# q in longer runs and another token order from batch 3 on, with an order of blocks 2 to 8 written out by hand: linear attention followed by a PReLU feed-forward layer

## The chip, the cores and the metric

The kernel runs on one core of a Trainium2 chip. The metric is the device time of one execution in microseconds (us); given are the median and the extremes of several runs. Five engines work side by side: TensorE (PE, matmuls; its weight loads are shown apart as PEld), VectorE (DVE), ScalarE (ACT), GpSimd (POOL) and SyncE (SP, which only issues DMAs here). A core has 16 DMA engines, which all queues share.

## The reference

Linear attention without a softmax, an RMS norm of each head's output row, and then two matrix products with a PReLU between them:

```python
batch, n_heads, seq, head_dim = (8, 8, 576, 64)
kv = np.einsum('bhsd,bhse->bhde', k, v)
out = np.einsum('bhsd,bhde->bhse', q, kv)
rms = np.sqrt(np.mean(out * out, axis=-1, keepdims=True) + 1e-06)
attn = out / rms * g_norm
x = attn.transpose(0, 2, 1, 3).reshape(B * S, H * D)   # 4608 tokens x 512
h = x @ w_in                                           # 512 -> 2048
g = np.maximum(h, 0.0) + alpha * np.minimum(h, 0.0)
out = g @ w_out                                        # 2048 -> 512, float32
```

The matmuls' operands are fp16, their sums float32.

## The kernel before

The 4,608 tokens are worked in nine blocks w of 512 (four tiles of 128 tokens, tile number 4w + i). A batch has 576 tokens, four tiles of 128 (`MAIN`, `TPP` = 4) and a remainder of 64 (`REM`), so tile and batch borders meet only every second batch. A tile that holds the end of one batch and the start of the next is computed with zero-padded halves (`PAD`).

For block w the steps have short names, which the hand-written order also uses. `ld.q.b.t`, `ld.k.b.t`, `ld.v.b.t` load the inputs of batch b through POOL's DMA queue, which turns float32 into fp16 on the way; t = 4 is the remainder. `q.b.t` is a DMA transpose on SP's queue (L400, `dma_t`) that brings q into `qt_sb` with the head dimension on the partitions, two heads above one another, as wide as the tokens. `kv.b` are the matmuls of k and v (L1337), `kvc.b` copies their PSUM result into `kv_masked` as fp16 (L1348, ACT; head 0 of a pair on partitions 0 to 63, head 1 on 64 to 127). `R.w.i` are the row matmuls of a pair of token tiles (`rows_mm`, L519; i = 1 for tiles 1 and 0, i = 3 for 3 and 2): out rows = q times kv, each matmul with 64 partitions of contraction, the two heads of a pair on the two partition halves. `q2`, `q3`, `rs` square and sum each row on ACT and take the root, `n` multiplies (DVE, L608), and `x.w.i` is a DMA transpose (L620) that makes the tile of `xt`, the moving operand of the first product. `M.w.u` are 16 tiles of h = x w_in (four 512-column matmuls each, L641; `Ma` and `M.w.0` split the first by columns), `r` and `s` the PReLU (ACT L650, DVE L656). From block 3 on half of the tiles go through a Strassen-like scheme of seven products (`f.w.s.n`, `t`, `a`). `p.w.n.k` are the products of the second layer (L895), again seven instead of eight, `S` their sums of operands, `y` the reading of the results, `st` the stores (POOL's queue, and SP's for `c12`).

Everything up to the end of `loop_one` stands in the program as written. From there on the steps are collected with their needs. `in_order` then emits, again and again, that step among the ready ones whose `place` is least: a number from the table `AT` plus 27.0 for each block. Each engine and each DMA queue works in the order in which its steps were emitted; the waits between engines follow from the tiles that the steps write and read. Every load of this part is preceded on POOL by `gate`, a copy of one element of the piece of `gt` (the PReLU's output) that was last emitted, so POOL waits for it and the load goes no earlier. Loads of k and v wait for one more such element, of a transposed tile.

For the batches 3 to 7 q is loaded by four DMAs of 128 tokens (L212, `load_q`): a token of a head is 64 numbers, so each run is 256 bytes in DRAM and 128 bytes in SBUF. There is one buffer for it from batch 3 on (`kept`), and the load of a piece waits for the transpose of the batch before that reads the same piece. The row bank in PSUM exists once from block 2's end on, so a row group or a kv group waits for the norms or the copy of the one before. The output of batches 3 to 7 is in token order: `quad_out` stores 256 tokens by 256 features in one DMA. Batches 0 to 2 (`B_NAT` = 3) already have another order of tokens, in which a partition holds consecutive tokens; `grid` gives their places in the output.

## Time and profile before

| | |
|---|---|
| median of 3 timed runs | 272.12 us |
| lowest and highest of them | 271.74 and 274.9 us |
| the profiled execution: its own time | 270.98 us |
| its span, first to last instruction | 269.2 us |
| granted clock of TensorE, share of full | 0.999 |
| DMA packets, of them under 512 bytes | 90,821; 62,996 |

The profile shows one execution. Its page gives each engine's busy time, the span in 40 slices, the DMA queues, the chain of waits that ended last and the costliest groups of instructions. Further views of the same trace answer for a stretch of time, for a tile, for one line of the code, or list the instructions in order of time. Durations of matmuls overlap, since they are pipelined: from start to start they are shorter than the duration that a row gives.

### The profile page before, as it was taken

What the parts mean: (1) busy time and instruction counts of PE and PEld (TensorE: products, weight loads), DVE (VectorE), ACT (ScalarE), POOL (GpSimd) and SP (SyncE); (2) the same over time, 40 slices, a digit from 0 to 9 for tenths busy, and PEclk for the clock granted to TensorE, in tenths of its full rate; (3) what the DMA queues carried; (4) which work ended last, traced back from release to release, by engine and by line L of the source; (5) the groups of instructions that cost most, each with busy time, mean ns of one, the idle gap of its engine ahead of it and who ended that gap; (6) DMA issues with size and microseconds to landing.
All of it is one profiled execution on the core that took longest, in us unless ns stands there. A gap on an engine that the chain in (4) does not pass through costs nothing.

```text
span 269.2 us, 6788 instructions
## 1 busy us (share of the span) xinstructions
PE 261.9 (97%) x2477; PEld 182.8 (68%) x2477; DVE 228.1 (85%) x437; ACT 191.8 (71%) x684; POOL 94.9 (35%) x166
## 2 busy tenths in 40 slices
PE   6999999999999999999999999999999999999994
PEld 2554454456556757885788678867885788678883
DVE  6559966899977888999889988998899989978962
ACT  2567637787579779879977997799779983757400
POOL 8853652513530326874346521804040003002100
PEclk9999999999999999999999999999999999999999
DMA  7999999995999899999999993999464013100413
GB/s 189 201 199 206 195 198 189 183 195 92 195 128 169 75 131 126 129 161 197 189 163 156 138 153 66 110 191 129 107 138 99 19 24 119 39 2 11 145 41 118
DMA packets 90821, 35.76 MB, mean 133 GB/s; under 512 B 62996, under 2 KB 88612, under 8 KB 90788
## 3 DMA queue, kind: packets, MB, share of 16 engines
q0 software_dynamic: 57104, 23.68, 68.5%
q1 hardware_dynamic: 32708, 10.63, 24.0%
q10 hardware_dynamic: 976, 1.02, 1.2%
q8 instruction: 19, 0.31, 0.5%
q14 instruction: 14, 0.11, 0.2%
HBM read 36.71 MB, written 9.44 MB: 171 GB/s over the span
## 4 chain that ended last, share of the span: by engine, by line
PE 85%; DMA 8%; ACT 2%; issue 2%; DVE 1%; SPq 1%; POOL 0%; POOLq 0%
PE h_ps L641 23%; PE yY L895 14%; PE yX L895 9%; PE yZ L895 8%; PE mY L1247 8%; PE y L686 5%; PE mV L1247 4%; DMA qt_sb<-qst 3%; PE h_ps L674 2%; DMA vst<-in_v_dram 2%; PE mX L1247 2%; PE or_ps L519 1%; DMA y_sb<-in_g_norm_dram 1%; DMA qst<-in_q_dram 1%; PE kv_ps L1337 1%
## 5 line engine op out<-in xcount | busy, mean ns | idle before, releaser
L641 PE MATMUL h_ps<-xt,w_in_sb 128*128 128x512 f16 x348 | 83.0, 379 | 0.1
L656 DVE SCALAR_TENSOR_TENSOR gt<-m_sb,beta_sb,h_ps 128x512 f16<-128x512 f32 x96 | 67.1, 741 | 4.6 <-ACT m_sb L650 3.6
L650 ACT ACTIVATE m_sb<-h_ps 128x512 f32<-128x512 f32 x96 | 55.0, 604 | 14.3 <-PE h_ps L641 11.9
L641 PEld LDWEIGHTS <-w_in_sb 128*128 128x128 f16 x348 | 33.1, 98 | 32.3 <-issue 0.3
L895 PEld LDWEIGHTS <-s 128*128 128x128 f16 x496 | 48.0, 98 | 8.4 <-DVE s L813 0.2
L895 PEld LDWEIGHTS <-gt 128*128 128x128 f16 x384 | 37.4, 98 | 8.6
L582 ACT ACTIVATE sq_sb<-or_ps 128x64 f16<-128x64 f32 x192 | 39.7, 286 | 2.2 <-PE or_ps L519 2.2
L582 ACT ACTIVATION_READ_ACCUMULATOR sq_sb<-or_ps 128x1 f32 x192 | 39.4, 273 | 0.0
L1402 POOL COPY gate_sb<-gt 1x1 f16<-1x1 f16 x39 | 10.5, 269 | 76.9 <-DVE gt L656 54.7
L895 PE MATMUL yX<-w_out_sb,gt 128*128 128x256 f16 x256 | 35.2, 273 | 0.0
L895 PE MATMUL yY<-wsum,s 128*128 128x256 f16 x256 | 32.9, 273 | 0.0
L698 POOL DMA_DIRECT2D out_dram<-y_sb x24 | 15.2, 639 | 45.8 <-ACT y_sb L957 42.8
L608 DVE TENSOR_TENSOR x_rows<-or_ps,rstd_r 128x512 f16<-128x512 f32 x27 | 17.4, 685 | 9.0 <-ACT rstd_r L592 8.8
L1314 DVE SCALAR_TENSOR_TENSOR gt<-m_sb,beta_sb,mh 128x256 f16<-128x256 f32 x48 | 20.5, 477 | 0.2 <-ACT m_sb L1307 0.2
L1307 ACT ACTIVATE m_sb<-mh 128x512 f32<-128x512 f32 x24 | 15.1, 629 | 6.3 <-DVE mh L1269 6.3
L1266 ACT COPY mu<-mY 128x512 f32<-128x512 f32 x24 | 14.1, 588 | 6.5 <-PE mY L1247 6.5
L1269 DVE TENSOR_TENSOR mh<-mV,mu 128x512 f32<-128x512 f32 x24 | 16.4, 685 | 2.5 <-ACT mu L1266 2.4
L212 POOL DMA_DIRECT2D qst<-in_q_dram x20 | 17.8, 891 | 2.2 <-issue 2.0
L686 PE MATMUL y<-w_out_sb,gt 128*128 128x512 f16 x64 | 16.3, 380 | 0.0
L895 PE MATMUL yZ<-wsum,s 128*128 128x256 f16 x120 | 16.2, 273 | 0.0
L895 PE MATMUL yY<-wsum,gt 128*128 128x256 f16 x128 | 15.5, 273 | 0.0
L1247 PEld LDWEIGHTS <-w_in_sb 128*128 128x128 f16 x144 | 14.1, 98 | 1.6
(150 smaller groups left out, 425.0 us busy)
## 6 DMA issues: line engine op xcount, KB each, us to landing
kst<-in_k_dram POOLq DMA_DIRECT2D x7, 512.0 KB, 7.7
vst<-in_v_dram POOLq DMA_DIRECT2D x6, 512.0 KB, 6.5
out_dram<-y_sb POOLq DMA_DIRECT2D x11, 256.0 KB, 3.2
qst<-in_q_dram POOLq DMA_DIRECT2D x20, 128.0 KB, 4.5
w_out_sb<-in_moe_w_out_dram POOLq DMA_DIRECT2D x8, 256.0 KB, 12.1
out_dram<-y_more POOLq DMA_DIRECT2D x5, 256.0 KB, 4.2
w_in_sb<-in_moe_w_in_dram POOLq DMA_DIRECT2D x2, 512.0 KB, 10.4
qst<-in_q_dram POOLq DMA_DIRECT2D x2, 512.0 KB, 10.7
```

The source lines that it names most:

```text
L212: nc.gpsimd.dma_start(out=stages[b, "q"][:, t, :, :], in_=srcs["q"][b, :, t * P : (t + 1) * P, :].rearrange("h p d -> p h d"),)
L582: nc.scalar.activation(out=sq[:, half, j], in_=o_ps[:, half, j], func=AF.Square, accum_out=ssq[:, half, j : j + 1],)
L608: nc.vector.tensor_tensor(out=xr[:].rearrange("p j h d -> p h j d"), in0=o_ps, in1=rstd[:].unsqueeze(3).to_broadcast([P, 2, NPAIR, D]), op ...
L641: nc.tensor.matmul(out=h_ps[:], lhsT=w_in_blk(c, g), rhs=xts[w][:, c, :], start=(c == 0), stop=(c == NC - 1),)
L650: nc.scalar.activation(out=neg[w, g][:], in_=h_ps[:], func=AF.Relu, scale=-1.0)
L656: nc.vector.scalar_tensor_tensor(out=gts[w, i][:, r, :], in0=neg.pop((w, g))[:], scalar=beta_sb[:, g : g + 1], in1=h_ps[:], op0=ALU.mult, ...
L686: nc.tensor.matmul(out=y[:], lhsT=gt_cols(w, g, a * P, (a + 1) * P), rhs=w_out_blk(g), start=(n == 1), stop=(n == NF),)
L698: engs[store_turn[0] % len(engs)].dma_start(out=dst, in_=src)
L895: nc.tensor.matmul(out=bank, lhsT=lhs, rhs=rhs, start=fresh, stop=(c == NK - 1), skip_group_check=True,)
L1247: nc.tensor.matmul(out=t[bank][:, r, :], lhsT=lhs[:, c, r * P : (r + 1) * P], rhs=rhs[:, c, :], start=(fresh and c == r == 0), stop=(c == ...
L1269: nc.vector.tensor_add(out=h_tile(t, what)[:, :, HW:W], in0=src[:], in1=u[:])
L1314: nc.vector.scalar_tensor_tensor(out=gts[w, i][:, r, cols], in0=m, scalar=beta_sb[:, g : g + 1], in1=h, op0=ALU.mult, op1=ALU.add,)
```

## The change

From batch 3 on a partition p holds the tokens 4p to 4p + 3 of the batch's first 512, for q as it already was for k and v. q is loaded by two DMAs of four heads each (`QL` = 2), in runs of four tokens: 1,024 bytes in DRAM, 512 bytes in SBUF. One DMA transpose then takes two heads with their four tokens, 512 columns; in its result a head and a pair of tokens make a piece of 128 columns, with the even token on partitions 0 to 63 and the odd one on 64 to 127. A row matmul of tokens t = 0 to 3 thus works on the partition half t modulo 2, whichever head it is. For that `kv_copy` writes kv of both heads to both halves: one copy of all 128 partitions and two that cross the halves. A pair of tiles whose tokens lie on different halves takes a PSUM bank for each tile, where it was one for each head; the matmuls are ordered so that the halves alternate where they can.

The row order of the blocks changes with it (`place_of`): odd batches from 3 on put their last 64 tokens first, so that these share a tile with the last 64 of the batch before, and every other tile lies in one batch with one t. A 64-token piece is a matmul of 64 rows of its own, in place of two padded ones of 128. A row group needs all four transposes of its batch. The stores of these batches follow the new order through `grid`; where two neighbouring tiles are not two neighbouring t of one batch, they leave in several DMAs.

The order of the steps is a list of 1,036 names, and `in_order` only walks it. A load can carry a mark: `@s.w.u` gates it by the piece of `gt` that was last emitted at the step s.w.u, `@-` by the one at the start, and `@!` sets no such gate. Two needs are added for operand sums that a later sum still reads (`read_by`, and one for `t`); they bear on the order alone.

```diff
...
             in_=srcs[nm][b, h0:h1, 0:MAIN, :].rearrange("h (p t) d -> p h (t d)", t=TPP),
         )
 
-    def load_q(b, t):
-        if (b, "q") not in stages:
-            stages[b, "q"] = stage_for(b, "q", [P, TPP, H, D])
-        nc.gpsimd.dma_start(
-            out=stages[b, "q"][:, t, :, :],
-            in_=srcs["q"][b, :, t * P : (t + 1) * P, :].rearrange("h p d -> p h d"),
-        )
+    QL = 2
+
+    def load_q(b, i):
+        load_main(b, "q", i * H // QL, (i + 1) * H // QL)
 
     def buf_of(b, nm):
         return bufs[b % (2 if nm == "q" else NBUF)][nm]
...
 
     def dma_t(b, ts=tuple(range(NT))):
         qt = qt_sb[b % 2][:, :, PAD : PAD + S]
-        for t in ts:
+        for t in ts if b >= B_NAT else ():
+            n = P if t < TPP else REM
+            if t == TPP:
+                src = rem_of(b, "q")[0:REM].rearrange("p h d -> p (h d)")
+            else:
+                src = stages[b, "q"][:, 2 * t : 2 * t + 2].rearrange("p h t d -> p (h t d)")
+            nc.sync.dma_start_transpose(
+                out=qt_flat(b)[:, t * W : t * W + NC * n].rearrange("p (c n) -> p c n", c=NC),
+                in_=src,
+            )
+        for t in ts if b < B_NAT else ():
             c0, c1 = t * P, min((t + 1) * P, S)
-            if t == TPP:
-                src = rem_of(b, "q")[0:REM]
-            else:
-                src = buf_of(b, "q")[:, t] if b < B_NAT else stages[b, "q"][:, t]
+            src = rem_of(b, "q")[0:REM] if t == TPP else buf_of(b, "q")[:, t]
             nc.sync.dma_start_transpose(
                 out=qt[:, :, c0:c1], in_=src.rearrange("p h d -> p (h d)"),
             )
-        for j in range(NPAIR):
+        for j in range(NPAIR if b < B_NAT else 0):
             qts[b, j] = qt_sb[b % 2][:, j, PAD : PAD + S]
+
+    def qt_flat(b):
+        return qt_sb[b % 2][:].rearrange("p j n -> p (j n)")
+
+    def place_of(b, r):
+        if b >= B_NAT and b % 2:
+            r = r - REM if r >= REM else r + MAIN
+        return divmod(r, P) if r < MAIN else (TPP, r - MAIN)
 
     def unit0(i):
         return ident16[i * P0 : (i + 1) * P0, i * P0 : (i + 1) * P0]
...
             xts[w] = xt_p.tile([P, NPAIR, W], FP16, name="xt")
         return xts[w][:, j, :]
 
+    def row_parts(w, i):
+        n0 = w * W + i * P
+        out, x = [], 0
+        while x < P:
+            b, r = divmod(n0 + x, S)
+            t, p = place_of(b, r)
+            n = min(P - x, REM if t == TPP else P)
+            out.append((b, t, slice(x, x + n)))
+            assert p == 0 or b < B_NAT
+            x += n
+        return out
+
+    def row_ops(w, i):
+        ops = []
+        for b, t, rows in row_parts(w, i):
+            for j in range(NPAIR):
+                for h in range(2):
+                    n = rows.stop - rows.start
+                    half = h if b < B_NAT or t == TPP else t % 2
+                    part = slice(half * D, (half + 1) * D)
+                    if b < B_NAT:
+                        r = w * W + i * P + rows.start - b * S
+                        lhs = qt_sb[b % 2][part, j, PAD + r : PAD + r + n]
+                        rhs = kvs[b, j][part, part]
+                    else:
+                        c = (
+                            TPP * W + j * REM if t == TPP
+                            else (2 * j + h) * 2 * P + t // 2 * P
+                        )
+                        lhs = qt_flat(b)[part, c : c + n]
+                        rhs = kvs[b][part, half ^ h, j, :]
+                    ops.append((half, h, rows, j, lhs, rhs))
+        return ops
+
     def rows_mm(w, tiles):
         o_ps = row_tile([2, 2, NPAIR, D], "or_ps")
+        ops = [row_ops(w, i) for i in tiles]
+        apart = all(len({y[0] for y in x}) == 1 for x in ops)
+        left = []
         for x, i in enumerate(tiles):
-            b, r = divmod(w * W + i * P, S)
-            for j in range(NPAIR):
-                if r + P <= S:
-                    steps = ((b, PAD + r),)
-                else:
-                    assert r + PAD == S
-                    steps = ((b, S), (b + 1, 0))
-                for n, (bb, c) in enumerate(steps):
-                    for h in range(2):
-                        part = slice(h * D, (h + 1) * D)
-                        nc.tensor.matmul(
-                            out=o_ps[:, h, x, j, :],
-                            lhsT=qt_sb[bb % 2][part, j, c : c + P],
-                            rhs=kvs[bb, j][part, part],
-                            start=(n == 0), stop=(n == len(steps) - 1), skip_group_check=True,
-                        )
-            ots[w, "r", i] = o_ps[:, :, x]
+            half = ops[x][0][0]
+            ots[w, "r", i] = o_ps[:, half] if apart else o_ps[:, :, x]
+            left += [(x, *op) for op in ops[x]]
+        if not apart:
+            left.sort(key=lambda y: y[3].stop - y[3].start)
+        was = None
+        while left:
+            n = next((n for n, y in enumerate(left) if was and y[1] != was[1]), 0)
+            x, half, h, rows, j, lhs, rhs = was = left.pop(n)
+            nc.tensor.matmul(
+                out=ots[w, "r", tiles[x]][rows, h, j, :], lhsT=lhs, rhs=rhs, start=True,
+                stop=True, skip_group_check=True,
+            )
 
     def cols_mm(w, i):
         b, r = divmod(w * W + i * P, S)
...
         i = 0
         while i < P:
             b, r = divmod(n0 + i, S)
-            np_, nt = (P0, T0) if b == 0 else (P, TPP)
-            if b < B_NAT and r < np_ * nt:
-                t, p = divmod(r, np_)
-                cnt = min(P - i, np_ - p)
+            t, p = divmod(r, P0) if b == 0 else place_of(b, r)
+            if b == 0 or t < TPP:
+                cnt = min(P - i, (P0 if b == 0 else P) - p)
                 yield i, cnt, b, t, p
             else:
-                cnt = P - i if b >= B_NAT else min(P - i, S - r)
-                yield i, cnt, None, n0 + i, 0
+                cnt = min(P - i, REM - p)
+                yield i, cnt, None, b * S + MAIN + p, 0
             i += cnt
 
     def grid(b):
...
 
     def quad_out(w, r, h, src, subs=(0, 1)):
         n0 = w * W + r * HW
-        if n0 >= B_NAT * S and len(subs) == 2:
-            put(
-                out[n0 : n0 + HW, h * HC : (h + 1) * HC].rearrange("(a p) m -> p a m", p=P),
-                src[:],
-            )
-            return
         one, two = list(row_pieces(n0)), list(row_pieces(n0 + P))
         if len(subs) == 2 and all(
             x[2] is not None and (*x[:3], x[3] + 1, x[4]) == y for x, y in zip(one, two)
...
             kvs[b, j] = kv_masked[:, b % 4, j, :]
 
     def kv_copy(b):
+        if b < B_NAT:
+            for i in range(2):
+                part = slice(i * D, (i + 1) * D)
+                nc.scalar.copy(out=kv_masked[part, b % 4, :, part], in_=kv_tiles[b][part])
+            return
+        kvs[b] = kv_masked[:, b % 4].rearrange("p j (x d) -> p x j d", x=2)
+        nc.scalar.copy(out=kvs[b][:, 0], in_=kv_tiles[b])
         for i in range(2):
-            part = slice(i * D, (i + 1) * D)
-            nc.scalar.copy(out=kv_masked[part, b % 4, :, part], in_=kv_tiles[b][part])
+            part, other = slice(i * D, (i + 1) * D), slice((1 - i) * D, (2 - i) * D)
+            nc.scalar.copy(out=kvs[b][other, 1], in_=kv_tiles[b][part])
 
     def row_kv(bs):
         for b in bs:
...
     def put_rows(w, tiles, free, used):
         needs = []
         for i in tiles:
-            b, r = divmod(w * W + i * P, S)
-            needs += [("q", b, t) for t in range(r // P, min((r + P - 1) // P, TPP) + 1)]
-            needs.append(("kvc", b))
-            if r + P > S:
-                needs += [("q", b + 1, 0), ("kvc", b + 1)]
+            for b, t, _ in row_parts(w, i):
+                needs += [("q", b, x) for x in ((TPP,) if t == TPP else range(TPP) if b >= B_NAT else (t,))]
+                needs.append(("kvc", b))
         rows = ("R", w, tiles[0])
         step(rows, "rows", lambda: rows_mm(w, tiles), (*free, *needs))
         for i in tiles:
...
         b = w + 1
         for t in range(NT if b < B else 0):
             step(("q", b, t), "turn", lambda t=t: dma_t(b, (t,)),
-                 (("ld", "q", b, t), *(("R", b - 1, i) for i in (1, 3))))
+                 (("ld", "q", b, t if t == TPP else t * QL // TPP), *(("R", b - 1, i) for i in (1, 3))))
         if w + 2 >= B:
             return
         for nm in "kvq":
...
 
     def put_load(nm, b):
         needs = (("kv", b - 1),) if nm != "q" else ()
-        for t in range(NT) if nm == "q" else (TPP, 0):
+        for t in (*range(QL), TPP) if nm == "q" else (TPP, 0):
             after = turns_before(nm, b) if t == 0 else ()
 
             def fn(t=t, after=after):
-                gate(gt_last[0])
+                for src in load_gate:
+                    gate(src)
                 for key in after:
                     gate(turned(*key))
                 if t == TPP:
...
                     load_q(b, t)
                 else:
                     load_main(b, nm)
-            own = (("q", b - 2 if t == TPP else b - 1, t),) if nm == "q" else ()
+            own = ()
+            if nm == "q":
+                n = TPP // QL
+                own = (("q", b - 2, t),) if t == TPP else tuple(("q", b - 1, n * t + i) for i in range(n))
             step(("ld", nm, b, t), "part" if t == TPP else "loadq" if nm == "q" else "load", fn, needs + own + after)
 
     def put_rest():
-    LOOP = 27.0
-    AT = {
...
-    def place(key):
...
+    ORDER = """
+        late.2.0 late.2.2 late.2.1 y.1.seed kv.3 Ma.2.0 kvc.3 S.1.1.3 ld.v.4.4@- M.2.2 S.1.1.0
...
+        y.1.c22 q3.3.3 S.2.3.1 p.2.1.3 rs.3.2 p.1.3.0 rs.3.3 n.3.2 r.2.13 M.2.14 y.2.p1 n.3.3 x.3.2
+        r.2.12 p.1.3.1 s.2.13 r.2.14 R.4.1 s.2.12 p.1.3.2 q2.4.0 x.3.3 p.1.3.3 s.2.14
+        ld.q.4.1@s.2.12 M.2.15 q2.4.1 y.1.c12 q.4.0 st.1.c22 p.2.2.0 r.2.15 p.2.2.1 q3.4.0 s.2.15
+        p.2.2.2 q.4.1 ld.q.4.4@! Ma.3.0 q3.4.1 S.2.1.1 p.2.2.3 st.1.c11 S.2.1.0 rs.4.0 M.3.1 rs.4.1
+        n.4.1 M.3.2 r.3.1 n.4.0 q.4.2 y.2.c11 s.3.1 kv.4 r.3.2 t.3.1 y.2.seed M.3.0 s.3.2 q.4.3
+        M.3.3 ld.k.5.4@s.2.11 r.3.0 ld.q.5.0@s.2.11 s.3.0 M.3.6 r.3.3 x.4.1 S.2.2.0 kvc.4 M.3.4
+        S.2.2.1 x.4.0 p.2.6.0 s.3.3 r.3.4 p.2.6.1 r.3.6 s.3.4 R.4.3 ld.q.5.1@s.3.3 p.3.1.0 q2.4.2
...
+        ld.k.6.0@! p.3.6.0 s.4.2 r.4.3 R.5.3 r.4.1 S.3.3.0 p.3.6.1 q2.5.2 M.4.6 s.4.4 ld.v.6.4@!
...
+        rs.6.2 y.4.u3 n.6.2 ld.q.7.1@! f.5.3.1 f.5.2.r22 f.5.2.3 x.6.2 f.5.2.r21 p.4.4.0 ld.q.7.0@!
+        f.5.2.c12 y.4.c11 p.4.4.1 S.5.3.1 p.4.4.2 f.5.3.seed st.4.c11 p.4.4.3 f.5.2.s11 f.5.3.2
+        y.4.c21 f.5.2.s22 R.7.1 f.5.2.r12 f.5.3.6 f.5.2.s21 f.5.3.5 f.5.3.u2 p.4.5.0 f.5.3.r11 q.7.4
+        f.5.3.7 f.5.3.s11 p.4.5.1 f.5.3.u3 Ma.6.0 q2.7.1 S.5.3.0 q.6.4 p.4.5.2 f.5.2.s12 q2.7.0
...
+        f.6.3.s12 M.7.1 n.8.1 r.7.3 y.5.c12 x.8.1 R.8.3 s.7.3 M.7.2 q2.8.2 s.7.0 x.8.0 M.7.7 r.7.1
...
     def in_order():
-
...
-        while todo:
-            bare = [s for s in todo if not s[1]]
-            s = bare[0] if bare else min((s for s in todo if usable(s)), key=lambda s: place(s[0])[0] + 1e-6 * rank[s[0]])
...
+        todo = {".".join(map(str, s[0])): s for s in steps if s[1]}
+        names, done, gates = {s[0] for s in steps if s[1]}, set(), {"-": gt_last[0]}
+        for x in ORDER:
+            name, _, at = x.partition("@")
+            s = todo.pop(name)
+            assert all(n in done or n not in names for n in s[3]), name
+            if at:
+                load_gate[:] = [gates[at]] if at != "!" else []
+            yield s[2]
+            done.add(s[0])
+            gates[name] = gt_last[0]
+        assert not todo
 
     for fn in in_order():
         fn()
```

More of the change, by code (lines that the diff above doesn't have):

```diff
@@ L626 @@
     gt_last = []
+    load_gate = []
     h_turn = [0]
@@ L1427, in load @@
         if nm == "q":
-            for t in range(TPP):
-                load_q(b, t)
+            for i in range(QL):
+                load_q(b, i)
             load_rem(b, "q")
@@ L1554, in used, with read_by @@
             return tuple(("p", w - 1, n, x) for x in ((k, k + 1) if pairs else (k,)))
+        def read_by(n, k):
+            return tuple(("S", w - 1, n, x) for x in ((k // 2,) if w > 2 else (k, k + 1) if pairs else (k,)))
         full = lambda f, k: f(k) + f(k + 1) if pairs else f(k)
@@ L1559, in put_m2 @@
                 sums(3, k, *full(lo, k), *used(7, k))
-            sums(1, k, *full(lo, k), *full(hi, k), *used(5, k))
-            sums(2, k, at(1, k), *used(6, k))
+            sums(1, k, *full(lo, k), *full(hi, k), *used(5, k), *read_by(2, k))
+            sums(2, k, at(1, k), *used(6, k), *read_by(4, k))
             sums(4, k, at(2, k), *used(3, k))
@@ L1703, in turned @@
             return xts[w][0:1, 0, i * P : i * P + 1]
-        return qt_sb[w % 2][0:1, 0, PAD + i * P : PAD + i * P + 1]
+        return qt_flat(w)[0:1, i * W : i * W + 1]
     def turns_before(nm, b):
@@ new lines @@
+    """.split()
+    def in_order():
+        todo = {".".join(map(str, s[0])): s for s in steps if s[1]}
[10 more added lines that the diff above has]
+        assert not todo
```

128 lines of the change are left out of this document (78 added, 50 removed), and 66 rows, old and new, of the table AT.

## The prediction

> **What bounds the kernel now.** I read the page first, for the engines' shares and the forty slices, and then the table of stretches, to see where the fullest engine is not full.
>
> ```profile
> span 269.2 us, 6788 instructions
> PE 261.9 (97%) x2477; PEld 182.8 (68%) x2477; DVE 228.1 (85%) x437; ACT 191.8 (71%) x684; POOL 94.9 (35%) x166
> PEclk9999999999999999999999999999999999999999
> ...
> 18.00:72.00 54.00, 53.99 (x435) 27.79 (x434) 46.59 (x87) 36.48 (x69) 23.07 (x34) 1.00 1.38 180
> 72.00:130.00 58.00, 56.96 (x575) 39.77 (x574) 50.16 (x90) 48.78 (x240) 26.81 (x51) 1.00 1.24 148
> 130.00:264.00 134.00, 134.00 (x1260) 106.19 (x1258) 119.72 (x226) 98.45 (x366) 30.77 (x55) 1.00 0.64 100
> ```
>
> In the last three rows the first number is the stretch's length and the second PE's busy time. From 18 to 264 us PE is idle for 0.01 + 1.04 + 0 = 1.05 us. A busy PE could still be a slow one, so next comes the chain of waits in order of time: start, duration, what.
>
> ```profile
> 96.83 4.35 DMA qt_sb<-qst
> 101.22 0.41 PE or_ps L519 x16
> ...
> 127.63 0.55 issue
> 128.17 0.53 PE or_ps L519 x24
> ...
> 131.86 1.73 PE h_ps L641 x8
> 138.39 1.75 PE yY L895 x16
> ```
>
> Eight matmuls of 512 columns in 1.73 us are 216 ns each, sixteen of 256 columns in 1.75 us are 109 ns: the same 0.42 ns a column for both, back to back at the full granted clock. So PE's matmul work itself sets the end from 18 us on. The DMA entries of this chain are long, but they only say who released PE; what they cost is PE's gap. PE's own order of time shows the gaps:
>
> ```profile
> 77.05 0.20 PE L519 MATMUL or_ps<-kv_masked,qt_sb 64*128 64x64 f16 x2
> 77.55 0.49 PE L519 MATMUL or_ps<-kv_masked,qt_sb 64*128 64x64 f16 x22 [0.29 <-DMA qt_sb<-qst]
> ...
> 99.18 1.90 PE L641 MATMUL h_ps<-xt,w_in_sb 128*128 128x512 f16 x8
> 101.22 0.41 PE L519 MATMUL or_ps<-kv_masked,qt_sb 64*128 64x64 f16 x16
> 101.56 0.61 PE L895 MATMUL yY<-wsum,s 128*128 128x256 f16 x4
> ```
>
> All three gaps stand before row matmuls (`rows_mm`, L519): 0.29 us at 77, 0.14 us at 101 (from the modelled end at 99.18 + 1.90) and 0.55 us at 128, together 0.98 of the stretch's 1.04 us. The first two end with a transpose of q, the third with nothing that the profile names.
>
> **The change, part by part.** *PE's matmuls.* The order holds the same products, M1 tiles and kv groups under the same names, so nothing is added or taken. The row matmuls keep their number too: 16 for a pair of tiles, 24 where a pair holds a batch's last 64 tokens. Sixteen take 101.22 to 101.56, 0.34 us or 21 ns each, while the two partition halves alternate. In the new layout a tile of 128 tokens lies on one half (its t modulo 2). Its partner in a pair lies on the other, so the alternation stays, except in two pairs, tiles 22 and 23 and tiles 30 and 31: there one tile's eight matmuls follow each other on the same half. No row of before shows that. From below: 21 ns again, no cost (or a little gain, as the 64-token pieces are half as wide). From above, a weight load that nothing overlaps:
>
> ```profile
> L519 PEld LDWEIGHTS <-qt_sb x240: 92/95/96, 54.2 to 208.8; 64*128 64x128 f16 x120
> ```
>
> 95 ns instead of 21, times 16, is 1.2 us. I take twice 21 ns, since the halves share the array two at a time in the nearest row: 16 x 21 ns = +0.3 us. [...]
>
> *ACT.* Each of five batches gets one more copy of kv, 128x256.
>
> ```profile
> L1348 ACT CAST kv_masked<-kv_ps 64x256 f16<-64x256 f32 x12 | 4.3, 361 | 0.2 <-PE kv_ps L1337 0.2
> L608 DVE TENSOR_TENSOR x_rows<-or_ps,rstd_r 128x512 f16<-128x512 f32 x27 | 17.4, 685 | 9.0 <-ACT rstd_r L592 8.8
> ```
>
> The same 256 elements a partition: 5 x 0.36 = 1.8 us of an engine that is busy for 98.45 of 134 us. What waits for it is the row group after kv; three copies take 1.08 us, and the new order puts 2.6 to 3.7 us of PE work between kv and that group (counted with the spacings above), so: nothing.
>
> *POOL.* q comes by two loads a batch instead of four, ten fewer. The gate copies of the ordered loads fall from 36 to 10 (the entries with a name or a dash behind the at sign). Ten stores more: three pairs of tiles (22-23, 26-27, 30-31), two feature halves each, leave in 3, 2 and 3 pieces instead of 1.
>
> ```profile
> L212 POOL DMA_DIRECT2D qst<-in_q_dram x20 | 17.8, 891 | 2.2 <-issue 2.0
> L698 POOL DMA_DIRECT2D out_dram<-y_sb x24 | 15.2, 639 | 45.8 <-ACT y_sb L957 42.8 <-DVE y_sb L963 3.0
> L1402 POOL COPY gate_sb<-gt 1x1 f16<-1x1 f16 x39 | 10.5, 269 | 76.9 <-DVE gt L656 54.7 <-DVE gt L1314 22.2
> ```
>
> -8.9 + 6.4 - 7.0 = -9.5 us on an engine that is 35% busy, worth nothing by itself. The 76.9 us that gates waited matter more: that pacing mostly goes, so loads start as early as their buffers allow.
>
> *q's transfers.* Runs of 512 bytes replace runs of 128: 5 x (4,096 - 1,024) = 15,360 fewer.
>
> ```profile
> kst<-in_k_dram POOLq DMA_DIRECT2D x7, 512.0 KB, 7.7
> qst<-in_q_dram POOLq DMA_DIRECT2D x20, 128.0 KB, 4.5
> qt_sb<-qst SPq DMA_TRANSPOSE x20, 3.7
> ...
> 91.92 0.87 POOL L212 DMA_DIRECT2D qst<-in_q_dram  x1 [0.73 <-issue]
> ...
> 95.03 0.88 POOL L212 DMA_DIRECT2D qst<-in_q_dram  x1
> ```
>
> Four q loads from 91.92 to 95.03 + 4.5 = 99.5 bring 512 KB in about 7.6 us, k's 512 KB in longer runs take 7.7: the rows show no penalty for the short runs, and I count no gain. [...]
>
> *The waits.* A row group of batch 3 on needs all four transposes of its batch, where it needed those of its own tokens. Counting PE work in the new order: the group at 77 us needs no more than the last 64 tokens of batch 3; the group at 128 us now stands 7.6 us of PE work behind the last transpose it needs. Their 0.29 + 0.55 us go. R.4.3 (the one at 101 us) has 9.4 us of PE work between its second load (`ld.q.4.1`) and itself. The chain: gate 0.27, load between 4.5 and 7.7 (128 and 512 KB; this one is 256), one more transpose's issue 1.2 (from this row of the transposes of q, shortest, median and longest in ns),
>
> ```profile
> L400 SPq DMA_TRANSPOSE qt_sb<-qst x20: 1189/1216/2017, 73.0 to 199.9; - x20
> ```
>
> and its landing 3.7: 9.7 to 12.9 us, so a wait of 0.3 to 3.5 us. Much below 0.3 is excluded only if the DMA queues are as full as now. I take 0.4, near the short end, because four back-to-back small loads moved 512 KB in the time of one. The old 0.14 us there gets a little larger.
>
> *The order.* PSUM: one row bank, so a group waits for the norms of the one before. kv.4 and R.8.3 stand with no PE step behind the last norm (n.4.0, n.8.1), each with one M1 tile (0.86 us) just ahead of it; a norm takes 0.685, so each wait is 0 to 0.69 us. I take 0.1 each, because the tile ahead covers the norm if DVE starts it on time. DVE's work is unchanged (119.72 busy of 134), and in the new order its listed work stays behind PE's or level with it. The head to 18 us and the tail from 264 us keep their steps.
>
> **Sum.** Profiled execution: 270.98 us, of which the span is 269.2 and 1.78 lies around it; -1.05 (gaps) + 0.3 + 0.4 + 0.2 = -0.15, so 270.8. The timed runs' median, 272.12, lies 1.14 above that execution, hence 272.12 - 0.15 = 272.0 us.
>
> **Rivals.** *All gaps go and none come.* For it: PE's clock and supply are full elsewhere. 272.12 - 1.05 = 271.1 us, still no change that can be told (2%, 5.4 us, is about what a measurement of this kernel can).
>
> *Slower: ungated loads delay the transposes of x and q.* One mechanism: without gates the 512 KB loads of a batch start together, and transposes queue among them. Landing of transposes of x, shortest, median, longest:
>
> ```profile
> DMA to landing us min/median/max: 2.4/2.9/7.7
> ```
>
> Places: block 3 (3.9 us of PE work from x.3.2 to Ma.3.0), block 6 (4.8 us from x.6.2 to Ma.6.0) and R.4.3. At the longest landing that is 3.8 + 2.9 + 3.5 = 10.2 us, 282 us; about two thirds of it, 6.5 us, gives 278.5. It decides once x lands later than 4.8 us after issue. For it: blocks 3 and 6 have load entries without a pace close by; against: the median is 2.9 us, and blocks 4, 5, 7 and 8 keep 10 us or more.
>
> *Faster by over 2%.* It would take 5.4 us from PE's path, and only 1.05 us of gaps and the 5.2 us after 264 exist. It needs fewer or quicker matmuls, which the edit doesn't have; or the transposes and their waits hold back more than the gaps show.
>
> **How the numbers follow.** Forecast with small waits: 0.5, 272.0 us. All gaps gone: 0.3, 271.1. Slower by load bursts: 0.17, 278.5, of which some 0.03 end within 2%. Faster: 0.03, 266. So faster 0.03, same 0.83, slower 0.14. The likely cases' own range goes from 272.12 - 1.05 - 1.14 (all gaps gone, timed like the profiled run) = 269.9 to 272.0 + 0.9 + 1.2 (the weight-load bound and the rest of both PSUM waits) + 3.1 (R.4.3's long end) = 277.2. Eight in ten: 269.6 to 277.4; it leaves out the worse part of the bursts and the gain.
>
> **What would show it.** Right: in the stretch 72:130 PE idle under 1.5 us, in 130:264 under 1; row matmuls still 21 ns apart outside the two pairs; POOL under 90 us busy. Wrong: a gap of PE ended by a transpose of x before the first M1 tile of block 3 or 6; a gap before R.4.3 of over 1 us; the eight one-half matmuls 95 ns or more apart; a PE slower than 109 ns for 256 columns; DVE idle time in front of norms that ends in PE gaps at kv.4 or R.8.3.

## The result, and the profile after

| | before | after |
|---|---|---|
| median of 6 timed runs, us | 272.48 (271.69 to 275.31) | 282.13 (278.59 to 285.19) |
| ratio to before, 95% interval | | 1.029 (1.023 to 1.035): slower |
| profiled execution, us | 270.98 | 278.59 |
| its span, us | 269.2 | 276.8 |

The profiled execution of after is the quickest of the six. The other five took 280.13 to 285.19 us at a granted TensorE clock of 0.993 down to 0.979, where the profiled one had 0.997; that difference is taken up where the prediction's size is discussed. The ratio leaves out disturbed executions on both sides, so it is smaller than that of the two medians (1.035).

The page of after:

```profile
span 276.8 us, 6684 instructions
PE 263.3 (95%) x2477; PEld 182.8 (66%) x2477; DVE 225.3 (81%) x437; ACT 192.6 (70%) x689; POOL 82.2 (30%) x140
DMA packets 75460, 35.75 MB, mean 129 GB/s; under 512 B 42516, under 2 KB 73252, under 8 KB 75428
```

The same table of stretches as before (stretch, length, busy time of PE, PEld, DVE, ACT, POOL, then granted clock, DMA share and GB/s):

```profile
18.00:72.00 54.00, 53.99 (x432) 27.51 (x431) 45.88 (x87) 36.54 (x69) 21.39 (x33) 1.00 1.31 179
72.00:130.00 58.00, 56.27 (x554) 39.52 (x552) 46.22 (x85) 47.19 (x227) 17.24 (x33) 1.00 1.21 144
130.00:264.00 134.00, 128.69 (x1209) 100.06 (x1208) 116.07 (x222) 100.44 (x381) 29.68 (x49) 1.00 0.55 96
```

The same 2,477 matmuls. From 72 to 264 us PE now idles for 1.73 + 5.31 = 7.04 us, against 1.04 before. Over the whole span its idle time grew from 269.2 - 261.9 = 7.3 to 276.8 - 263.3 = 13.5 us, by 6.2 of the 7.6 us; the other 1.4 are busy time of PE, 0.3 of them in the row matmuls (see What held), the rest not traced. PE's own order of time shows three gaps that hold most of it:

```profile
102.80 0.29 PE L567 MATMUL or_ps<-kv_masked,qt_sb 64*128 64x64 f16 x8
104.52 0.44 PE L567 MATMUL or_ps<-kv_masked,qt_sb 64*128 64x64 f16 x8 [1.43 <-DMA qt_sb<-qst]
...
147.88 0.60 PE L1286 MATMUL mV<-xt,vst 128*128 128x256 f16 x4
150.06 1.02 PE L687 MATMUL h_ps<-xt,w_in_sb 128*128 128x512 f16 x4 [1.57 <-issue]
...
173.92 0.60 PE L940 MATMUL yZ<-wsum,s 128*128 128x256 f16 x4
177.88 0.81 PE L720 MATMUL h_ps<-xt,w_in_sb 128*128 128x384 f16 x4 [3.36 <-DVE s L856]
```

They stand inside R.4.3 (102 us, a transpose of q), before M.5.1 (150 us) and before Ma.6.0 (177 us): both of the latter are the first tiles that read x of a new block. Ahead of the second and the third the two queues run like this (POOL's and SP's order of time, start, duration, what):

```profile
133.04 0.91 POOL L204 DMA_DIRECT2D kst<-in_k_dram  x1 [0.34 <-PE yX L940]
...
137.00 0.82 POOL L204 DMA_DIRECT2D qst<-in_q_dram  x1
...
137.91 0.90 POOL L204 DMA_DIRECT2D vst<-in_v_dram  x1
...
139.63 2.99 SPq L665 DMA_TRANSPOSE xt<-x_rows  x2
...
166.62 0.90 POOL L204 DMA_DIRECT2D kst<-in_k_dram  x1
...
168.21 3.26 SPq L665 DMA_TRANSPOSE xt<-x_rows  x2
...
169.73 1.51 POOL L204 DMA_DIRECT2D qst<-in_q_dram  x2 [2.22 <-issue]
```

For those of block 5 the trace gives landing times:

```
us            issued   landed   from issue to landing
kst           133.04   139.59    6.55
qst           137.00   143.02    6.02
vst           137.91   148.46   10.55
xt (x.5.2)    139.63   148.34    8.71
xt (x.5.3)    141.36   149.97    8.61
```

Block 5's x was handed to the DMA engines 1.7 us behind v of batch 6 and landed with it. In block 6 k of batch 7 left 1.6 us ahead of x.6.3, and the two loads of q follow x.6.2 (169.57) by 0.2 and 0.9 us; the landings of these two transposes are not recorded.

x.5.2 landed 0.12 us ahead of v of batch 6, a 512 KB load, and x.5.3 1.51 us behind it. That the load holds these 128 KB transposes up is inferred from that; how it does so no run shows, and e5 below tests whether it does.

In before the two blocks differ from each other. SP, POOL and PE:

```profile
134.02 0.88 POOL L204 DMA_DIRECT2D vst<-in_v_dram  x1 [0.34 <-issue]
134.30 4.23 SPq L620 DMA_TRANSPOSE xt<-x_rows  x2
...
145.23 0.82 PE L674 MATMUL h_ps<-xt,w_in_sb 128*128 128x384 f16 x4
...
161.92 2.52 SPq L620 DMA_TRANSPOSE xt<-x_rows  x2
...
168.55 0.89 POOL L204 DMA_DIRECT2D vst<-in_v_dram  x1 [1.05 <-PE mY L1247]
...
172.25 0.82 PE L674 MATMUL h_ps<-xt,w_in_sb 128*128 128x384 f16 x4
```

For block 6 both loads of batch 7 (v here, k at 171.22) come behind x, which lands 2.4 to 3.0 us after its issue where a landing is recorded, and PE's first reader, Ma.6.0 at 172.25, stands 9.0 us behind the last transpose (163.23). In after that distance is 5.0 us (169.57 to 174.52, where the gap begins). For block 5 v of batch 6 leaves ahead of the last two transposes in before as well (134.30 and 137.09); k comes at 140.44, and the first reader stands 8.1 us behind the last transpose, in after 7.1 (141.36 to 148.49, where the gap begins).

### The profile page after: what moved, and what is told of

The parts are those of the page before. It is cut to its first block, busy times and chain, and to the rows that moved or that the text cites. A ratio compares the mean times of both kernels' runs of the same rounds, so it can differ in the third digit from the quotient of the medians.

```text
span 276.8 us, 6684 instructions
## 1 busy us (share of the span) xinstructions
PE 263.3 (95%) x2477; PEld 182.8 (66%) x2477; DVE 225.3 (81%) x437; ACT 192.6 (70%) x689; POOL 82.2 (30%) x140
## 4 chain that ended last, share of the span: by engine, by line
PE 81%; DMA 7%; ACT 5%; DVE 4%; issue 2%; SPq 1%; POOL 0%; DVEq 0%; ACTq 0%
PE h_ps L687 25%; PE yY L940 12%; PE yX L940 9%; PE yZ L940 9%; PE mY L1286 6%; PE y L732 5%; DMA vsb<-in_v_dram 3%; PE mV L1286 3%; ACT sq_sb L627 3%; PE h_ps L720 2%; DMA qt_sb<-qst 2%; PE or_ps L567 2%; PE kv_ps L1376 2%; PE mX L1286 2%; DMA y_sb<-in_g_norm_dram 1%
## 5 line engine op out<-in xcount | busy, mean ns | idle before, releaser
L687 PE MATMUL h_ps<-xt,w_in_sb 128*128 128x512 f16 x348 | 84.1, 379 | 1.6 <-issue 1.6
L702 DVE SCALAR_TENSOR_TENSOR gt<-m_sb,beta_sb,h_ps 128x512 f16<-128x512 f32 x96 | 69.3, 745 | 14.0 <-ACT m_sb L696 13.2
L687 PEld LDWEIGHTS <-w_in_sb 128*128 128x128 f16 x348 | 33.2, 98 | 32.8 <-issue 2.1
L940 PE MATMUL yX<-w_out_sb,gt 128*128 128x256 f16 x256 | 36.6, 273 | 0.0
L940 PE MATMUL yY<-wsum,s 128*128 128x256 f16 x256 | 34.3, 273 | 0.0
L744 POOL DMA_DIRECT2D out_dram<-y_sb x31 | 18.4, 597 | 46.0 <-ACT y_sb L996 42.1
L940 PE MATMUL yY<-wsum,gt 128*128 128x256 f16 x128 | 16.7, 272 | 0.5 <-ACT u L988 0.5
L204 POOL DMA_DIRECT2D qst<-in_q_dram x12 | 9.5, 791 | 26.0 <-DMA qt_sb<-qst 19.6
L1448 POOL COPY gate_sb<-gt 1x1 f16<-1x1 f16 x13 | 3.0, 228 | 47.5 <-DVE gt L702 47.5
L744 POOL DMA_DIRECT2D out_dram<-y_more x11 | 6.6, 609 | 34.9 <-ACT y_more L996 31.9
```

What stands on the lines that cost most here:

```text
L687: nc.tensor.matmul(out=h_ps[:], lhsT=w_in_blk(c, g), rhs=xts[w][:, c, :], start=(c == 0), stop=(c == NC - 1),)
L702: nc.vector.scalar_tensor_tensor(out=gts[w, i][:, r, :], in0=neg.pop((w, g))[:], scalar=beta_sb[:, g : g + 1], in1=h_ps[:], op0=ALU.mult, ...
L744: engs[store_turn[0] % len(engs)].dma_start(out=dst, in_=src)
L940: nc.tensor.matmul(out=bank, lhsT=lhs, rhs=rhs, start=fresh, stop=(c == NK - 1), skip_group_check=True,)
```

## The experiments

"After" stands for the changed kernel; times are medians, ratios are to the kernel before in the same series, with their 95% intervals.

| kernel | us | ratio |
|---|---|---|
| e1: after, gates back | 277.92 | 1.023 (1.018 to 1.028) |
| e2: after, four loads listed later | 277.56 | 1.022 (1.015 to 1.028) |
| e3: after, second q load of batch 4 earlier | 282.84 | 1.038 (1.031 to 1.045) |
| e4: layout alone, planner's order | 288.45 | 1.060 (1.053 to 1.068) |
| e5: after, four loads held until x has landed | 272.76 | 1.003 (1.001 to 1.006) |
| e6: order alone, layout of before | 283.95 | 1.045 (1.039 to 1.051) |
| e7: e5, R.4.3 3 us later | 273.28 | 1.005 (1.003 to 1.008) |
| e8: e5, R.4.3 1.75 us later | 272.46 | 1.002 (0.999 to 1.004) |
| e9: e5 in block 6 alone | 275.48 | 1.013 (1.010 to 1.016) |
| e10: e5 in block 5 alone | 281.87 | 1.034 (1.029 to 1.039) |
| e11: e8, two more loads moved | 272.35 | 1.002 (1.000 to 1.005) |

### Is it the missing gates, the place in the list, or the layout? (e1 to e4)

e1:

```diff
-                load_gate[:] = [gates[at]] if at != "!" else []
+                load_gate[:] = [gt_last[0] if at == "!" else gates[at]]
```

> The kernel after, with a gate on the latest gate tile put back in front of every ordered load (the exclamation entries); list of the order unchanged. Theory 1, the missing gates let the loads start together: with them back the landing of the transposes of x falls to about 3 us, the gaps of PE at 148 us (1.7) and 174 us (3.5) go, and the time is 272 to 275. Theory 2, the place in the list sets the time of a load and not the gate, since the loads of after were issued within 1 to 3 us of the PE work beside which they are listed: the gaps stay, 278 to 283.

Between the two theories: 277.92 us. The gap at 148 us is gone (x of block 5 landed at 146.9 and 147.4, just in time), the one before Ma.6.0 is not. e1, PE's order of time:

```profile
171.38 0.60 PE L940 MATMUL yZ<-wsum,s 128*128 128x256 f16 x4
175.67 1.07 PE L720 MATMUL h_ps<-xt,w_in_sb 128*128 128x384 f16 x4 [3.69 <-DVE s L856]
176.53 1.06 PE L940 MATMUL yZ<-wsum,s 128*128 128x256 f16 x4
177.39 1.06 PE L940 MATMUL yX<-w_out_sb,gt 128*128 128x256 f16 x4
```

A gate on the last gate tile holds a load until VectorE has come that far, but nothing ties that tile to the transposes: k of batch 7 still left at 166.28, between x.6.3 (165.67) and x.6.2 (167.03), and landed at 175.79, where PE starts again (175.67). And each group of four matmuls of 256 columns behind the gap takes 0.86 us instead of 0.44: half clock (the page of e1 gives 7 tenths for the slice from 172.4 to 179.3 us and 9 for every other).

e2 (the entries are taken from their old places, which are not shown):

```diff
-        p.3.7.3 x.5.2 f.4.2.3 n.5.3 y.3.u3 p.4.1.1 f.4.2.r21 f.4.2.c12 p.3.4.0 x.5.3 f.4.3.1
+        p.3.7.3 x.5.2 f.4.2.3 n.5.3 y.3.u3 p.4.1.1 f.4.2.r21 f.4.2.c12 p.3.4.0 x.5.3 ld.v.6.0@! f.4.3.1
...
-        rs.6.2 y.4.u3 n.6.2 ld.q.7.1@! f.5.3.1 f.5.2.r22 f.5.2.3 x.6.2 f.5.2.r21 p.4.4.0 ld.q.7.0@!
+        rs.6.2 y.4.u3 n.6.2 f.5.3.1 f.5.2.r22 f.5.2.3 x.6.2 ld.q.7.1@! ld.q.7.0@! ld.k.7.0@! f.5.2.r21 p.4.4.0
```

> The kernel after, with four entries moved and nothing else: the load of v of batch 6 behind the last transpose of x of block 5 (x.5.3), the load of k and the two loads of q of batch 7 behind the last one of block 6 (x.6.2). Theory 2 (a transpose lands when the loads issued ahead of it have landed, so the listed place decides): x of blocks 5 and 6 lands within about 4 us, the gaps at 148 us (1.7) and at 174 us (3.5) go, PE is idle 2 to 3 us between 18 and 264, and the time falls by 5 us or more, to 273 to 277. Theory 1 (missing gates as such): the loads still start without a gate, so at most one of the gaps goes, 279 to 282. Theory 3, the gap at 174 us belongs to VectorE, whose last pair sum ends just before it: that gap stays, 279 to 281.

277.56 us lies between the theories, and both gaps are still there (2.05 and 2.00 us). e2, POOL and SP:

```profile
139.46 0.90 POOL L204 DMA_DIRECT2D vst<-in_v_dram  x1
...
141.46 3.52 SPq L665 DMA_TRANSPOSE xt<-x_rows  x2
```

v is listed behind x.5.3 and yet leaves 2.0 us ahead of x.5.2. The list orders each engine's own instructions. POOL has nothing left to wait for and runs ahead; SP waits for the norms. In block 6 it is the loads of q that run ahead: they leave at 168.82 and 171.08, x.6.3 and x.6.2 at 170.53 and 171.81, and k, now behind both, at 172.39. The gap there does not need k ahead of x. So a place in the list without a wait does not hold a load, and a gate at the old place does not hold it long enough: theories 1 and 2 each fail by half.

e3:

```diff
-        ld.q.4.1@s.2.12 M.2.15 q2.4.1 y.1.c12 q.4.0 st.1.c22 p.2.2.0 r.2.15 p.2.2.1 q3.4.0 s.2.15
+        M.2.15 q2.4.1 y.1.c12 q.4.0 st.1.c22 p.2.2.0 r.2.15 p.2.2.1 q3.4.0 s.2.15
...
-        s.2.8 x.3.0 p.1.5.3 r.2.10 p.2.1.2 q2.3.3 S.1.4.2 M.2.13 s.2.10 q3.3.2 S.1.4.0 M.2.12
+        s.2.8 x.3.0 p.1.5.3 r.2.10 p.2.1.2 q2.3.3 S.1.4.2 M.2.13 ld.q.4.1@s.2.11 s.2.10 q3.3.2 S.1.4.0 M.2.12
```

> The kernel after, with one entry moved: the second load of q of batch 4 stands some 6 us of PE work earlier, behind M.2.13 with the gate s.2.11 instead of s.2.12. If the gap of 1.6 us before the row group R.4.3 is only the chain load, transposes, row group, it goes, and 1.6 us of the time with it: about 280.5. If the transposes there wait for other transfers, the gap stays above 1 us and the time is 282.

The gap inside R.4.3 went, so it was that chain. But the load and the stores queued behind it now ran ahead of x.3.2, which landed 5.0 us after its issue instead of 2.5, and a new gap came before Ma.3.0 (e3, PE):

```profile
96.37 0.81 PE L720 MATMUL h_ps<-xt,w_in_sb 128*128 128x384 f16 x4 [0.76 <-DMA xt<-x_rows]
```

PE came to block 5 0.66 us earlier than in after, and both later gaps were longer than that accounts for (3.01 and 5.35 us, against 1.57 and 3.36), with a lower clock behind each (the page of e3 gives 7 tenths for the slice from 148.6 us, 6 and 8 for the two from 176.9): 282.84 us, no gain.

e4 takes the new layout with the planner, the due times and the gate before every load of the kernel before:

```diff
-    ORDER = """
...
+    LOOP = 27.0
+    AT = {
...
+                load_gate[:] = [gt_last[0]]
                 yield s[2]
```

> The new layout alone: q by two loads, transposed two heads at a time, kv on both partition halves, as in the kernel after; the order, and a gate before every load, come from the planner of the kernel before, with its due times. If the new order makes the slowdown: 270 to 274, no change. If the layout makes it (a row group that needs all transposes of its batch, one more copy of kv, pairs on one half): 277 or more, with gaps before row groups.

It is the slowest kernel of all, with gaps before row groups. What ended PE's waits in e4 (us in total, times, longest):

```profile
PE or_ps L567 <- DMA qt_sb<-qst: 6.7, 3, 6.0
PE or_ps L567 <- DMA qt_sb<-qsb: 5.8, 3, 2.8
```

The due times of before were set for row groups that read only their own tokens; in the new layout a group needs all four transposes of its batch and, in odd batches, the 64 remaining tokens first (the second line). So with these due times the layout loses 16 us. This says nothing yet about a layout with a fitting order.

### Held until x has landed (e5, e9, e10), and the order alone (e6)

e5, where `turned` names an element that the transpose of x writes, so that the gate waits for its landing:

```diff
-                load_gate[:] = [gates[at]] if at != "!" else []
+                load_gate[:] = [turned("x", *map(int, at[2:].split("."))) if at[0] == "x" else gates[at]] if at != "!" else []
...
-        p.3.7.3 x.5.2 f.4.2.3 n.5.3 y.3.u3 p.4.1.1 f.4.2.r21 f.4.2.c12 p.3.4.0 x.5.3 f.4.3.1
+        p.3.7.3 x.5.2 f.4.2.3 n.5.3 y.3.u3 p.4.1.1 f.4.2.r21 f.4.2.c12 p.3.4.0 x.5.3 ld.v.6.0@x.5.3 f.4.3.1
...
+        x.6.2 ld.k.7.0@x.6.2 ld.q.7.1@x.6.2 ld.q.7.0@x.6.2 f.5.2.r21 p.4.4.0
```

> The kernel after, with four loads bound to the transposes that they got ahead of: v of batch 6 waits on GpSimd for the landing of x.5.3, k and q of batch 7 for that of x.6.2 (a gate that reads the transposed x), each listed behind it. In e2 the same loads were listed there without a gate, and GpSimd issued v of batch 6 2 us ahead of x.5.2 all the same. If loads ahead in time are the cause: x of block 5 lands by about 145 us and x of block 6 by 173, the gaps at 148 us (1.7) and 174 us (3.5) go, the gap at R.4.3 (1.7) stays, and the time is 273 to 276. If the gap at 174 us belongs to VectorE or ScalarE: it stays above 2 us, 277 to 280.

272.76 us, 0.3% above before and a little below the forecast. The gap at R.4.3, which was to stay, is 0.87 us here instead of 1.43, though nothing was changed there. e5, the stretches:

```profile
72.00:130.00 58.00, 56.81 (x572) 39.76 (x570) 46.74 (x84) 47.85 (x228) 17.31 (x33) 1.00 1.17 145
130.00:264.00 134.00, 133.64 (x1253) 105.19 (x1252) 120.32 (x230) 100.17 (x380) 31.02 (x53) 1.00 0.54 100
```

PE's idle time from 130 to 264 us fell from 5.31 to 0.36. x of block 5 landed at 144.4 and 145.1, before PE asked for it. SP issued it within 0.6 us of the times of after (139.04 and 141.08), so it is the loads that changed, not the start of the transposes.

e6 is the kernel before with the new list in place of its planner; each of the two q loads of a batch stands for two of its four:

```diff
-        ld.q.4.0@s.2.1
+        ld.q.4.0@s.2.1 ld.q.4.1@s.2.1
```

> The order alone: the layout of the kernel before (q in four loads of 128-byte runs, one token tile a transpose, two copies of kv), with the list of the kernel after; each of its two q loads of a batch stands for two of the four. If the order makes the gaps at 148 and 174 us, they are here too, and q in small runs adds to the backlog: 277 to 284. If the order needs the new layout only for R.4.3, the gap there is under 0.5 us. If the new layout made the gaps: 271 to 274.

Without any of the new layout the gaps are here again, 2.36 us before M.5.1 and 4.60 before Ma.6.0, and one of 2.21 inside R.7.3, ended by a transpose of q: 283.95 us. At R.4.3 there is none. e6, PE:

```profile
149.06 1.02 PE L642 MATMUL h_ps<-xt,w_in_sb 128*128 128x512 f16 x4 [2.36 <-issue]
...
178.14 1.12 PE L675 MATMUL h_ps<-xt,w_in_sb 128*128 128x384 f16 x4 [4.60 <-issue]
```

So the order makes the two long gaps; the one at R.4.3 comes only with the new layout.

e9 and e10 take the two halves of e5's edit alone.

> Half of e5: the kernel after with only the loads of k and q of batch 7 held until x.6.2 has landed; v of batch 6 is as in the kernel after. If the two places add up and each gap also costs PE its clock for a while (in e1 the matmuls of 256 columns took 213 ns instead of 109 for 3.3 us behind a gap of 3.9 us): the gap at 174 us goes, that at 148 us stays at 1.7 to 3.2, and the time is 275 to 278. If block 6 alone carries it: 272 to 274.

> The other half of e5: only the load of v of batch 6 held until x.5.3 has landed. The gap at 148 us goes, that at 174 us stays at 3 to 5 us, with a stretch of half clock behind it in some executions: 276 to 279. If block 5 alone carries it: 272 to 274. The two halves together should save what e5 saves, 9.4 us.

e9 (block 6) took 275.48 us, as forecast; e10 (block 5) 281.87, above its forecast. Against before, after stands at 1.029, e9 at 1.013, e10 at 1.034 and both together (e5) at 1.003: block 5's half saves nothing alone, and 1% on top of block 6's. They do not add up, and e10 shows why. Its PE:

```profile
171.87 0.60 PE L940 MATMUL yZ<-wsum,s 128*128 128x256 f16 x4
179.09 1.44 PE L720 MATMUL h_ps<-xt,w_in_sb 128*128 128x384 f16 x4 [6.61 <-issue]
180.32 1.06 PE L940 MATMUL yZ<-wsum,s 128*128 128x256 f16 x4
...
184.53 0.81 PE L687 MATMUL h_ps<-xt,w_in_sb 128*128 128x512 f16 x3
```

and its stretches behind the gap (the granted clock stands third from the right):

```profile
179.00:182.40 3.40, 3.31 (x14) 2.05 (x15) 0.00 (x0) 0.00 (x0) 0.00 (x0) 0.50 0.23 52
182.40:186.00 3.60, 3.60 (x22) 2.41 (x20) 1.57 (x4) 1.71 (x4) 0.00 (x0) 0.71 0.00 0
```

With block 5's gap gone, PE comes to block 6 2.05 us earlier (171.87 against 173.92) but cannot start Ma.6.0 any earlier (179.09 against 177.88): the gap there grows from 3.36 to 6.61 us. (Why it starts 1.2 us later still is open; x's landing is not recorded here either.) Behind it PE runs at half clock: from Ma.6.0 to the next M1 tile it takes 184.53 - 179.09 = 5.44 us, in e9 177.39 - 174.56 = 2.83. So the gap costs another 2.6 us. e9 without that gap, PE and VectorE:

```profile
174.12 0.60 PE L940 MATMUL yZ<-wsum,s 128*128 128x256 f16 x4
174.56 0.81 PE L720 MATMUL h_ps<-xt,w_in_sb 128*128 128x384 f16 x4
...
177.39 0.81 PE L687 MATMUL h_ps<-xt,w_in_sb 128*128 128x512 f16 x3
...
176.91 0.68 DVE L856 TENSOR_TENSOR s<-gt 128x1024 f16<-128x1024 f16 x1
```

This also settles who released Ma.6.0. The profile of after names VectorE's sum (L856). In e9 the same sum runs at 176.91, 2.35 us after Ma.6.0 has started: PE never needed it. It was merely the last to end before the gap did. That Ma.6.0 waits for x is inferred: x's landing is not recorded in that trace, but the gap goes when the loads issued around x are held.

### Can the rest be had? (e7, e8, e11)

e7 and e8 list R.4.3 later on top of e5, e7:

```diff
-        S.2.2.1 x.4.0 p.2.6.0 s.3.3 r.3.4 p.2.6.1 r.3.6 s.3.4 R.4.3 ld.q.5.1@s.3.3 p.3.1.0 q2.4.2
-        t.3.2 p.2.6.2 s.3.6 f.3.2.1 t.3.3 q3.4.2 ld.k.5.0@! M.3.5 S.2.3.0 f.3.2.seed p.2.6.3 r.3.5
+        S.2.2.1 x.4.0 p.2.6.0 s.3.3 r.3.4 p.2.6.1 r.3.6 s.3.4 ld.q.5.1@s.3.3 p.3.1.0 t.3.2 p.2.6.2
+        s.3.6 f.3.2.1 t.3.3 ld.k.5.0@! M.3.5 R.4.3 q2.4.2 S.2.3.0 f.3.2.seed p.2.6.3 q3.4.2 r.3.5
```

and e8:

```diff
-        S.2.2.1 x.4.0 p.2.6.0 s.3.3 r.3.4 p.2.6.1 r.3.6 s.3.4 R.4.3 ld.q.5.1@s.3.3 p.3.1.0 q2.4.2
-        t.3.2 p.2.6.2 s.3.6 f.3.2.1
+        S.2.2.1 x.4.0 p.2.6.0 s.3.3 r.3.4 p.2.6.1 r.3.6 s.3.4 ld.q.5.1@s.3.3 p.3.1.0
+        t.3.2 p.2.6.2 R.4.3 q2.4.2 s.3.6 f.3.2.1
```

> e5 with the row group R.4.3 and its two squares listed 3 us of PE work later, behind M.3.5. If the 1.7 us before R.4.3 are a wait for the transposes of q alone, and nothing else is late there: the gap goes too, PE idles under 2 us between 18 and 264 us, and the time is 1.5 to 2 us below e5's, 271 to 274, level with the kernel before. If x of block 4 then comes late: a new gap before Ma.4.0 of 1 us or more, no gain over e5.

> e5 with R.4.3 and its first squares 1.75 us of PE work later (behind p.2.6.2), not 3 us as in e7, where ScalarE then had the squares, the relu and the copy u together and PE waited 1.4 us for u. If the two ends meet: no gap of more than 0.5 us before R.4.3 and none for u, 271.5 to 272.3, level with the kernel before or 0.3% below it. If ScalarE's queue moves with the row group whatever its place: 272.8, as e5.

e7's gap before R.4.3 is gone, but ScalarE, which waits 2.33 us for the row group with everything else behind it, then makes its copy u late, and PE waits 1.22 us for it: 273.28 us. e8 leaves 0.79 us at R.4.3 and 0.28 at two copies u: 272.46. e11 goes at that rest:

```diff
-        ld.q.4.1@s.2.12
+        ld.q.4.1@s.2.13
...
-        M.3.3 ld.k.5.4@s.2.11 r.3.0
+        M.3.3 r.3.0
...
-        q2.4.2 s.3.6
+        q2.4.2 ld.k.5.4@s.2.11 s.3.6
```

> e8 with two loads moved around R.4.3: the second load of q of batch 4 waits on s.2.13 instead of s.2.12 (about one M1 tile earlier), and the last 64 tokens of k of batch 5 stand behind R.4.3 instead of ahead of the transposes of q. If the 0.95 us left before R.4.3 are the backlog ahead of these transposes: the gap falls under 0.4 us, PE's gaps between 72 and 130 us add up to 0.5 us or less, and the time is 271.6 to 272.2. If x.3.2 and x.3.3 are delayed instead, a gap opens before Ma.3.0 at 95 us, as the 0.92 us in e3: 272.4 or more.

R.4.3's gap is gone and there is none at Ma.3.0, yet the time is the same, 272.35. PE of e11 further on:

```profile
154.48 0.32 PE L1376 MATMUL kv_ps<-vst,kst 128*64 128x64 f16 x8 [0.77 <-DMA ksb<-in_k_dram]
```

PE comes earlier to kv.6, whose inputs are now the late ones. No version beat the kernel before: e8 and e11 are level with it, and with PE idle for only 1.05 us between 18 and 264 us in before there was little more than that to win.

## Why the prediction was wrong

*The step that failed* is a wait put at nothing: the sum has no term for the transposes of x. The slower rival, which has one, was set aside with "against: the median is 2.9 us", a landing time from the trace of before. Even there 6 of the 21 landings recorded for x took 5.2 to 7.7 us, and no gap of PE ended with them; and the new list puts large loads close to x of blocks 5 and 6 and leaves PE less work until it reads them. In after x of block 5 landed 8.6 to 8.7 us after its issue, and Ma.6.0 started 8.3 us after that of x.6.2 (169.57 to 177.88), above the 4.8 from which the rival "decides". These two waits are 1.57 + 3.36 = 4.93 us.

For R.4.3 the bracket of 0.3 to 3.5 us held, the choice near its short end did not: 1.43. The load of q took 5.4 us (93.65 to 99.01), and the two transposes behind it landed 5.4 and 4.3 us after issue, not 3.7: 11.0 us (to 104.67) against 9.4 of PE work.

*The rival's places* were half right. Block 6 and R.4.3 are among them. Block 3 showed no gap. Block 5 was ruled out because "blocks 4, 5, 7 and 8 keep 10 us or more". That holds up to Ma.5.0; in the new list M.5.1 reads x first, 3.25 us ahead of it (150.06 and 153.31). That leaves 7.1 us from the last transpose for one that landed in 8.6: 1.5 us short, the gap of 1.57.

*Its cause* was half right too. "Without gates" is not the whole of it: with all gates back (e1) block 6 keeps its gap. For block 6 before had both loads behind x and 9.0 us of work in hand, where after has k ahead and 5.0. For block 5 before, too, had v ahead of two transposes, but k later and 1 us more in hand. How much is in hand decides as much as the landing: in after x.4.2 took 9.6 us (111.17 to 120.79) and was still in time for Ma.4.0 at 121.48, with no gap. Holding the loads is enough (e5); whether more work between x and its reader would do as well was not run.

*Its size*, 6.5 us, is near the 7.6 us between the two profiled executions, in part by luck: block 3's 3.8 us, which it counted, did not come, and block 5's 1.57, which it left out, did. From the median, 282.13, its 278.5 is further off, and no term stood for the clock: behind gaps of 3.69 us (e1) and 6.61 us (e10) PE ran at half rate for a while, which cost 1.7 us in e1 (4.06 us for what takes 2.39 in e9) and 2.6 in e10. The profiled execution of after had none of that behind its gap of 3.36 us. The other five were not profiled. An estimate, span times the missing share of the clock, gives 0.8 us for the profiled one and 2.0, 2.5 and 3.9 for those of 280.13, 282.01 and 282.26 us: 1.1 to 3.1 of the 1.5 to 3.7 us by which these are longer. What made the rest is open.

*What held.* The gaps at 77 and 128 us went as said. The row matmuls stay 21 ns apart; in the two pairs on one half the eight of one tile are 29 ns apart, and the group of 24 takes 0.61 us to the next matmul's start (130.25 to 130.86) where it took 0.46 in before (128.17 to 128.63): 0.15 us each, together the 0.3 forecast. The upper bound of 1.2 us, 0.9 above the 0.3 taken, did not come: a weight load of these matmuls takes 95 ns in after too (L567, median), and the eight on one half follow each other after 29, less than one such load. ACT's extra copy took 0.37 us and no wait of PE ends with it. POOL's busy time fell by 12.7 us (9.5 forecast) and the DMA packets by 15,361 (15,360 forecast); neither shows in the time, since e5, which has nearly all of both, is level with before. No gap came at kv.4 or R.8.3: the 0.2 us for PSUM was not needed. With the loads held, the layout and the order come out where the forecast stood (e5, 272.76 against 272.0).

*Left open:* how much k and how much the two q loads of batch 7 delay x of block 6 (held only together; in e2, with k behind x, 2.00 us of the gap stayed), and how much faster e4's layout would be with due times fitted to it.

## What to carry to other kernels

A transfer's landing time in a profile is the price under the pacing of that kernel (a transpose of x landed in at most 7.7 us in before, 9.6 in after); when a change touches the pacing, count the bytes that the new order puts ahead of each small transfer, and compare that with the PE work left until its first reader, whichever tile reads first. A place in a list of instructions ordered nothing between two engines here (in e2 v, listed behind x.5.3, left 2.0 us ahead of x.5.2): to keep a big load behind a small transfer, let it wait for the landing of that transfer. And test repairs together, since a gap removed made PE arrive earlier at the next late transfer (0.66 us in e3, 2.05 in e10; in e11 it then waited 0.77 us for inputs of kv.6).

## What the runs showed of the hardware

- *Some gaps had a second price.* Behind gaps of 3.69 us (e1) and 6.61 us (e10) PE ran at half clock for about 3.3 and 5.4 us (granted clock 0.50 from 179.0 to 182.4 us in e10); behind that of 3.36 us in after, and behind those of 2.8 us and less (e2, e4, e6, e9), it did not. In e3 a gap of 3.01 us was followed by one tile at full rate and then by half rate, seen at the 256-column products (a row of eight of them takes 1.70 us there, 1.04 at the full rate):

```profile
150.83 1.02 PE L687 MATMUL h_ps<-xt,w_in_sb 128*128 128x512 f16 x4 [3.01 <-issue]
...
152.29 1.91 PE L687 MATMUL h_ps<-xt,w_in_sb 128*128 128x512 f16 x4
154.00 1.70 PE L940 MATMUL yZ<-w_out_sb,s 128*128 128x256 f16 x8
```

So a gap of 3.36 us was followed by no drop and one of 3.01 us by one: the length of the gap alone did not decide it, and what else did is not shown.
- *A DMA transpose of 128 KB landed in 2.4 us where little else moved, and in 6.3 to 9.6 where a 512 KB load had been issued 0.8 to 3.9 us ahead of it.* The first are x from 185 to 200 us in after (2.40 to 2.44, at 80 GB/s and a DMA share of 0.38), the second x of block 5 in after (8.6 and 8.7, at 193 GB/s and 1.43 from 138 to 150 us) and in e1, and x.4.2 in after: 9.6 us, issued 0.84 us behind a load of v that itself took 9.8.
